# Fewer unread products ahead of one pair's scores, a third rectified tile, and scaling and reciprocal set apart, in a top-k attention kernel with a highway layer

## The chip, the cores and the metric

The kernel runs on one core of one Trainium2 chip. The metric is the device time of one execution in microseconds (us). Before the change it is 817.38 us, the median of three runs (813.4, 817.38 and 819.01). A core has five engines that work side by side, each through its own list of instructions: TensorE (PE in the profile; PEld is its weight load), VectorE (DVE), ScalarE (ACT), GpSimd (POOL) and SyncE (SP), which here only issues DMAs. They wait for one another through semaphores.

## The reference

There are 8 batches of 8 heads, 576 rows, head width 64. Each score row keeps its 32 largest entries, goes through a softmax, and is multiplied with the values. The heads of a row then form a vector of 512, which goes through a highway layer.

```python
scores = scale * np.matmul(q, k.transpose(0, 1, 3, 2))
kth = np.partition(scores, -top_k, axis=-1)[..., -top_k:-top_k + 1]
scores = np.where(scores >= kth, scores, -1000000000.0)
scores = scores - np.max(scores, axis=-1, keepdims=True)
attn = np.exp(scores)
attn = attn / (np.sum(attn, axis=-1, keepdims=True) + 1e-09)
x = np.matmul(attn, v)                    # then heads side by side: 4608 x 512
H = np.maximum(x @ w_h, 0.0)
T = 1.0 / (1.0 + np.exp(-(x @ w_t + b_t)))
out = T * H + (1.0 - T) * x
```

## The kernel before, in words

**Units, pairs and blocks.** The 576 rows of a batch are four full tiles of 128 rows and a last one of 64. A unit is one head of a full tile, or two heads of the last rows, stacked to 128 partitions. Two units make a pair, 18 pairs a batch: 16 of full tiles (numbers 0 to 15) and 2 of the last rows (16 and 17). There are 144 pairs in all. Four pairs make a full block, 128 rows of all eight heads; the two last-row pairs make one block of half the width.

**A step.** `step(i)` writes out, engine by engine, what is done in step i; each engine works through its instructions in the order in which they are written. Several pairs are in flight. In step i:

- PE adds the mask to the scores of pair i (`mask_add`, L409), multiplies the masked weights of pair i−3 with the values (`values`, L493), issues `spare(8)` (L277), and then the scores of pair i+2 (`scores`, L308 and L317 for full tiles, L325 and L334 for last rows). Behind these come part of a block's projections (`project`, L521, L523, L531) or transposes of the next batch's inputs (L249), and `spare(4)` or `spare(10)`.
- DVE takes the maxima of segments of pair i+1 (`segs`, L352), then the remaining maxima of pair i (`below`, L419, twice). Then it narrows the threshold down (`refine`, from L365 to L381), finds the 32nd value (L425, L438), and makes the masked weights of pair i−1 in `masked(0)` (L449) and `masked(1)` (L459, or L464 without help of POOL).
- ACT makes the comparison of one unit of the pair before (L442), may rectify or gate a projection (L606, L630) or copy transposes (L250), copies the accumulator out (`xs_copy`, L507), makes the exponentials (L415), copies scores (L347), and makes the masks (L396), which need the threshold of L381.
- POOL multiplies the hits (L435), makes biases (`biases`, L390) and one comparison (L453), and takes from a queue `pool_work` the scaling of a block (L562), two additions (L607, L608) and a product (L621). It issues DMAs: values for the next batch, casts of a block (L579), and `do_add` (L691), which adds the product tile to the sum of L607 by an accumulating DMA.
- SP issues the transposing DMAs of masked weights (L480) and of blocks (L584), loads and stores.

**Unread products.** `spare(n)` issues n products of constants into a part of the accumulator tile that nobody reads. The tile, `pso`, has one buffer: once four units' values are in it, `back_xs` has ACT copy it out and takes the tile anew, and the next products into it wait for that copy. `po["n"]` is the number of columns filled, 0 right after a copy.

**Scores.** Their PSUM tile has two buffers, so the scores of pair i+2 overwrite those of pair i, which DVE reads last in the second L419 of step i.

**The rectified tile.** `hh()` projects a block and writes the rectified result with ACT into the tile `h2` (named `h` in the profile). POOL uses it at L607 and L608, the product at L621 writes into it, and the accumulating DMA of L691 reads it. It comes from a pool of two buffers.

**Scaling and reciprocal.** When a block's heads are complete, `norm()` is put in the list `norms`, and `step` calls it at the end, behind `masked(1)` and the biases: DVE scales the sums (L556) and takes the reciprocal in place (L557). It also puts the block's scaling by L562 into `pool_work`. The biases of POOL are held behind `masked(1)` by an explicit dependence (`after`). A second path behind the main program, with exact maxima, runs only when a check at the end asks for it; it calls `norm()` too (L1099).

Of the kernel before, what the change touches and what calls it, by code (L numbers as in the profile page):

```python
# [11 lines left out]
FP32 = mybir.dt.float32  # L12
# [14 lines left out]
def kernel(  # L27
# [11 lines left out]
    P = nc.NUM_PARTITIONS  # L39
    B, H, S, D = q.shape  # L40
    dm = H * D
# [5 lines left out]
    nfull = S // P  # L47
# [11 lines left out]
    units = []  # L59
# [7 lines left out]
    pairs = [(u, u + 1) for u in range(0, NU, 2)]  # L67
    NG = len(pairs)
# [8 lines left out]
    etpool = ctx.enter_context(tc.tile_pool(name="et", bufs=6))  # L77
    xpool = ctx.enter_context(tc.tile_pool(name="x", bufs=3))
    fpool = ctx.enter_context(tc.tile_pool(name="f", bufs=2))
    xps = ctx.enter_context(tc.tile_pool(name="xps", bufs=2, space=bass.MemoryType.PSUM))  # L80
    ops = ctx.enter_context(tc.tile_pool(name="ops", bufs=1, space=bass.MemoryType.PSUM))
    fps = ctx.enter_context(tc.tile_pool(name="fps", bufs=1, space=bass.MemoryType.PSUM))
# [190 lines left out]
    def spare(n):  # L273
        if "t" not in po:
            po.update(t=pso_tile(), n=0)
        for _ in range(n):
            nc.tensor.matmul(  # L277
                po["t"][:, 4 * DE : BANK],
                ident_b[:],
                cst[:, 0 : BANK - 4 * DE],  # L280
                start=True,
                stop=True,
                skip_group_check=True,
            )
# [218 lines left out]
    def pso_tile():  # L503
        return ops.tile([P, BANK], FP32, tag="po", name="pso")
# [9 lines left out]
    def shape_of(qt):  # L514

        return (H, n_g, dm) if qt < nfull else (H // 2, n_g // 2, dm // 2)
# [31 lines left out]
    def ffn_pieces(b, qt, xs):  # L548
        nh, ng, w = shape_of(qt)
        st = dict(b=b, qt=qt, xs=xs)  # L550
        blocks.append(st)

        def norm():
            xs3 = xs[:, 0 : nh * DE].rearrange("p (h e) -> p h e", e=DE)
            rinv = cpool.tile([P, H], FP32, name="rinv")
            nc.vector.tensor_scalar(rinv[:, 0:nh], xs3[:, :, D], 1e-9, 2.0, ALU.add, ALU.mult)  # L556
            nc.vector.reciprocal(rinv[:, 0:nh], rinv[:, 0:nh])  # L557
            x = xpool.tile([P, dm], FP32, name="x")
            st["x"] = x

            def scaled(e):
                e.tensor_tensor(  # L562
                    x[:, 0:w].rearrange("p (h d) -> p h d", h=nh),
                    xs3[:, :, 0:D],
                    rinv[:, 0:nh].unsqueeze(2).to_broadcast([P, nh, D]),
                    ALU.mult,
                )
                if by_dma:
                    casts.append(cast)
                else:  # L570
                    ready.extend([xt, hh, tt])

            pool_work.append((scaled, w))

        by_dma = isinstance(b, int) and units[-1][0:2] > (b, qt + 2)

        def cast():
            xb = xpool.tile([P, dm], BF16, name="xb")
            nc.gpsimd.dma_start(xb[:, 0:w], st["x"][:, 0:w])  # L579
            return partial(turn, xb)  # L580

        def turn(xb):
            st["xT"] = fpool.tile([P, n_g, P], BF16, name="xT")
            nc.sync.dma_start_transpose(st["xT"][:, 0:ng, :], xb[:, 0:w])  # L584
            flying.append(b)
            ready.extend([hh, tt])

        def xt():
            ps = fps.tile([P, 512], FP32, tag="fp", name="fp")
            for g in range(ng):  # L590
                nc.tensor.transpose(ps[:, g * P : (g + 1) * P], st["x"][:, g * P : (g + 1) * P], ident_f[:])
            xT = fpool.tile([P, n_g, P], BF16, name="xT")
            st["xT"] = xT
            psv = ps[:].rearrange("p (g j) -> p g j", j=P)
            return lambda: nc.scalar.copy(xT[:, 0:ng, :], psv[:, 0:ng, :])

        def hh():
            ps = fps.tile([P, 512], FP32, tag="fp", name="fp")
            project(ps, qt, st["xT"], wh, False)
            h2 = fpool.tile([P, dm], FP32, name="h2")  # L600
            s1 = xpool.tile([P, dm], FP32, name="s1")
            st["h2"], st["s1"] = h2, s1
            x = st["x"]

            def evac():
                nc.scalar.activation(h2[:, 0:w], ps[:, 0:w], AF.Relu)  # L606
                pool_work.append((lambda e: e.tensor_add(s1[:, 0:w], h2[:, 0:w], x[:, 0:w]), w))  # L607
                pool_work.append((lambda e: e.tensor_sub(h2[:, 0:w], h2[:, 0:w], x[:, 0:w]), w))  # L608

            return evac  # L610

        def tt():
            ps = fps.tile([P, 512], FP32, tag="fp", name="fp")
            project(ps, qt, st["xT"], wt, True)
            if by_dma:
                flying.pop()
            t = fpool.tile([P, dm], FP32, name="tt")
            h2, s1 = st["h2"], st["s1"]

            def gated(e):  # L620
                ins = e.tensor_mul(h2[:, 0:w], h2[:, 0:w], t[:, 0:w])  # L621
                if e is nc.gpsimd:
                    adds.append((s1[:, 0:w], h2[:, 0:w], partial(store, b, qt, s1)))
                else:
                    e.tensor_add(s1[:, 0:w], s1[:, 0:w], h2[:, 0:w])
                    store(b, qt, s1)
                return ins

            def evac():
                nc.scalar.activation(t[:, 0:w], ps[:, 0:w], AF.Tanh)  # L630
                pool_work.append((gated, w))

            return evac

        return norm
# [21 lines left out]

    def blk_diff(k, ps):
        w = shape_of(k["qt"])[2]
        k["d"] = fpool.tile([P, dm], FP32, name="h2")  # L660
        nc.vector.scalar_tensor_tensor(
            out=k["d"][:, 0:w], in0=ps[:, 0:w], scalar=0.0, in1=k["x"][:, 0:w], op0=ALU.max, op1=ALU.subtract
        )
# [35 lines left out]
    norms = []  # L699
# [41 lines left out]
    po = {}  # L741
# [30 lines left out]
    def step(i):  # L772
# [31 lines left out]
        if back:  # L804
            back_pv(j)
            back_xs(j)
            st.pop(j)
        spare(8)
        ev = prep_filler() if to_prep and (i <= SPB or (len(to_prep) > 15 - k_in or len(layers) > 2) and i % 2) else None
        do_work(nc.gpsimd, 2 * dm if prev and ps_["r"][1] is None else dm)  # L810
        segs(i + 1, 2 * NSEG)
# [25 lines left out]
        def masked(s):  # L837
            if not prev:
                return None
            u = pu[s]  # L840
            if ps_["r"][s] is not None:
                ep, ins = (keep_min, keep_mul)[s](u, ps_["e"][s], ps_["r"][s])
            else:
                ep, ins = keep(u, ps_["sc"][s], ps_["e"][s])
            ps_["et"][s] = transposes(ep)
            return ins
# [20 lines left out]
        masked(0)  # L867
        for _ in ra:
            pass
        last = masked(1)  # L870
        if live:
            after(biases(i + 1), last)
        if norms:
            norms.pop(0)()
        if nxt:
            masks_of(i + 1)
        while turns and turns[0][0] <= i and len(flying) < 2:
# [166 lines left out]
    with tc.If(fine < 1):  # L1044
        with tc.For_i(0, B, 1) as bi:
# [26 lines left out]
            for pr in pairs[0 : NG // B]:  # L1072
                scs = copy_scores(scores(pr, prep)[2])
                ets = []
                for s, u in enumerate(pr):
                    b, qt, heads = units[u]
                    if heads[0] == 0:
                        xs = xpool.tile([P, H * DE], FP32, name="xs")
                    sc = scs[s]
                    w = cpool.tile([P, 32], FP32, name="gw")  # L1080
                    cur = sc
                    for r in range(TOP_K // 8):
                        nc.vector.max(w[:, r * 8 : r * 8 + 8], cur)
                        if r < TOP_K // 8 - 1:
                            nxt = gpool.tile([P, S], FP32, tag="gs", name="gs")
                            nc.vector.match_replace(nxt[:], w[:, r * 8 : r * 8 + 8], cur, -3.0e38)
                            cur = nxt[:]
                    nc.vector.tensor_copy(kth(u), w[:, TOP_K - 1 : TOP_K])
                    nc.vector.tensor_scalar_mul(tb(u), w[:, 0:1], -scale)
                    ep, _ = keep(u, sc, expo(u, sc))  # L1090
                    ets.append(transposes(ep))
                pso = pso_tile()
                n, r0 = values(pr, ets, vb, pso, 0), row_of(pr)
                if units[pr[0]][1] < nfull:
                    xs_copy(units[pr[0]][2][0], n, pso, xs)
                else:
                    xs_copy(0, n, pso, xs, r0, r0 + P2)
                if heads[-1] == H - 1:
                    ffn_pieces(bi, qt, xs)()  # L1099
                    do_work(nc.vector, NG * dm)  # L1100
                    while ready:
                        ready.pop(0)()()
                        do_work(nc.vector, NG * dm)
# [30 lines left out]
```

## Time and profile before

| | us |
|---|---|
| median of three runs | 817.38 |
| lowest and highest | 813.4 and 819.01 |
| the profiled execution, its own time | 818.4 |
| its span, first to last instruction | 816.7 |
| POOL busy | 559.3 |
| idle time of PE ahead of L277, for the copy of L507 | 40.0 in 70 waits |

The granted clock of TensorE was 0.993 of full speed over the span. A row of a timeline gives the start in us, the duration, engine and line, the tiles as out<-in, how many instructions are merged, and in brackets the idle time of the engine before the first and what ended it. A row of the chain gives the start, the duration and what ran; the chain is followed back from the last instruction to whatever released each one. A row of the waits reads "who <- whom: total us, times, longest".

### The profile page before, as it was taken

Reading aid. Unit: us, or ns where it says so; the run is one execution under the profiler, and the core shown is the slowest. Engines: PE = TensorE matmul, PEld = TensorE weight load, DVE = VectorE, ACT = ScalarE, POOL = GpSimd, SP = SyncE. Lnnn points to the kernel's source line nnn. Section 1 sums busy time; section 2 is a strip of 40 time slices with the busy share of each in tenths; the row PEclk is TensorE's granted clock in tenths of the full one; section 3 lists DMA queues with packets and bytes.
Section 4 is the critical chain, followed back from the end, with each engine's and each line's share of the span. In section 5 each row is a group of like instructions: output and inputs, shape, how many; then the busy total and the mean of one; then the engine's idle time right before and its main releaser. Section 6 shows DMA issues by size and latency. Waiting matters only on the chain.

```text
span 816.7 us, 20679 instructions
## 1 busy us (share of the span) xinstructions
PE 694.4 (85%) x6405; PEld 500.2 (61%) x6499; DVE 776.2 (95%) x4020; ACT 758.8 (93%) x1401; POOL 559.3 (68%) x712
## 2 busy tenths in 40 slices
PE   7889988888878888888888888888888888888884
PEld 5666766566655666566665666556656566565562
DVE  6999999999999999999999999999998999998995
ACT  5999999999999999999999998999999999998984
POOL 2666867777677766787667777677776776675750
PEclk9999999999999999999999999999999999999998
DMA  6799957985798657997679866697767975565553
GB/s 121 85 147 155 130 117 136 156 130 80 146 150 145 108 94 137 152 137 115 101 149 147 127 110 117 134 157 126 107 122 128 163 114 92 94 110 96 101 93 87
DMA packets 346359, 100.37 MB, mean 123 GB/s; under 512 B 330624, under 2 KB 338432, under 8 KB 346240
## 3 DMA queue, kind: packets, MB, share of 16 engines
q1 hardware_dynamic: 291024, 79.16, 53.0%
q0 software_dynamic: 53536, 19.34, 22.4%
q8 instruction: 53, 0.87, 0.4%
q10 hardware_dynamic: 1680, 0.46, 0.3%
q14 instruction: 66, 0.54, 0.2%
HBM read 31.72 MB, written 9.44 MB: 50 GB/s over the span
## 4 chain that ended last, share of the span: by engine, by line
ACT 37%; DVE 31%; PE 23%; DMA 4%; issue 3%; POOL 2%; SPq 0%; ACTq 0%; DVEq 0%; POOLq 0%
ACT m L396 14%; DVE wall L419 10%; DVE cand L352 9%; ACT e L415 7%; PE pso L277 6%; ACT sc L347 6%; ACT r L442 4%; PE xs L325 4%; DVE ep L449 3%; PE xs L308 3%; PE pso L493 2%; ACT xs L507 2%; DMA s<-h 2%; PE xs L409 2%; PE fp L521 2%
## 5 line engine op out<-in xcount | busy, mean ns | idle before, releaser
L352 DVE MAX8 cand<-xs 128x8 f32<-128x96 f32 x1728 | 297.1, 246 | 13.4 <-PE xs L334 7.4
L277 PE MATMUL pso<-cst,ident_b 128*128 128x252 bf16 x1881 | 253.1, 274 | 42.4 <-ACT xs L507 40.0
L453 POOL TENSOR_SCALAR ro<-sc,wall 128x576 bf16<-128x576 f32 x135 | 232.6, 1723 | 0.0
L277 PEld LDWEIGHTS <-ident_b 128*128 128x128 bf16 x1881 | 178.1, 98 | 82.1 <-issue 49.1
L415 ACT ACTIVATE e<-sc,be 128x576 bf16<-128x576 f32 x288 | 226.0, 785 | 0.1
L419 DVE MAX8 wall<-xs 128x8 f32<-128x576 f32 x288 | 204.0, 748 | 11.5 <-PE xs L409 5.0
L308 PE MATMUL xs<-kT,qT 64*128 64x256 f32 x1024 | 146.1, 402 | 31.9 <-DVE high L365 28.3
L347 ACT COPY sc<-xs 128x1152 f32<-128x1152 f32 x144 | 160.8, 1116 | 0.7 <-DVE cand L352 0.6
L308 PEld LDWEIGHTS xs<-kT,qT 64*128 64x128 f32 x1024 | 93.5, 187 | 62.9 <-issue 38.1
L435 POOL TENSOR_TENSOR hit<-hit,wall 128x18 f32<-128x18 f32 x143 | 32.4, 226 | 137.0 <-DVE hit L425 129.4
L396 ACT ACTIVATE m<-xs,wall 128x576 int8<-128x576 f32 x144 | 107.3, 745 | 20.0 <-DVE wall L381 17.8
L396 ACT ACTIVATE m<-sc,wall 128x576 int8<-128x576 f32 x144 | 111.3, 773 | 0.0
L409 PE MATMUL xs<-m,ident_b 128*128 128x64 bf16 (+1 forms) x507 | 92.0, 274 | 21.4 <-ACT m L396 19.4
L442 ACT ACTIVATE r<-sc,be 128x576 bf16<-128x576 f32 x143 | 109.8, 768 | 0.0
L409 PEld LDWEIGHTS <-ident_b 128*128 128x128 bf16 x576 | 51.7, 98 | 49.8 <-issue 29.3
L493 PEld LDWEIGHTS <-et 128*128 128x128 bf16 (+1 forms) x1600 | 68.9, 100 | 19.3 <-issue 3.8
L493 PE MATMUL pso<-vb,et 128*128 128x65 bf16 (+1 forms) x1600 | 74.6, 194 | 4.9 <-DMA et<-ep 0.3
L390 POOL TENSOR_TENSOR be<-wall,fac 128x4 f32<-128x4 f32 x144 | 29.1, 202 | 71.3 <-DVE ep L459 42.4
L449 DVE TENSOR_TENSOR ep<-e,r 128x576 bf16<-128x576 bf16 x143 | 64.5, 451 | 0.2 <-ACT r L442 0.2
L317 PEld LDWEIGHTS xs<-kd,qT 128*128 128x128 f32 x256 | 38.1, 188 | 42.7 <-issue 42.2
L317 PE MATMUL xs<-kd,qT 128*128 128x128 f32 x256 | 62.5, 326 | 0.0
L459 DVE TENSOR_TENSOR ep<-e,ro 128x576 bf16<-128x576 bf16 x135 | 60.5, 448 | 0.0
(127 smaller groups left out, 1024.1 us busy)
## 6 DMA issues: line engine op xcount, KB each, us to landing
kin<-in_k_dram SPq DMA_DIRECT2D x64, 128.0 KB, 3.0
qin<-in_q_dram SPq DMA_DIRECT2D x62, 128.0 KB, 3.2
out_dram<-s SPq DMA_DIRECT2D x30, 256.0 KB, 2.8
s<-h POOLq DMA_DIRECT2D x29, 256.0 KB, 4.1
et<-ep SPq DMA_TRANSPOSE x286, 3.4
xb<-x POOLq DMA_DIRECT2D x30, 128.0 KB, 3.1
vb<-in_v_dram POOLq DMA_DIRECT2D x28, 128.0 KB, 4.7
vb<-in_v_dram POOLq DMA_DIRECT2D x24, 64.0 KB, 3.2
```

What stands on the lines that cost most here:

```text
L277: nc.tensor.matmul(po["t"][:, 4 * DE : BANK], ident_b[:], cst[:, 0 : BANK - 4 * DE], start=True, stop=True, skip_group_check=True,)
L308: nc.tensor.matmul(ps[:, mo + n0 : mo + n0 + 256], qT[r : r + D, hp, qs : qs + P], kT[r : r + D, hp, n0 : n0 + 256], start=(n0 == 0), stop ...
L317: nc.tensor.matmul(ends, qT[:, hp, qs : qs + P], kd[:, hp, :], start=True, stop=True)
L347: nc.scalar.copy(sc[:], both)
L352: nc.vector.max(cand[:, s, :], sc[:, s * SEG : (s + 1) * SEG])
L396: nc.scalar.activation(m1[:].bitcast(I8)[:, 1 : 2 * S : 2], ps, AF.Sign, bias=wall[:, u, THR : THR + 1], scale=ABOVE, accum_out=csum[:, u ...
L409: nc.tensor.matmul(ps[:, s0:s1], ident_b[:], m1[:, s0:s1], start=False, stop=True, skip_group_check=True)
L415: nc.scalar.activation(e[:], sc, AF.Exp, bias=tb(u), scale=scale)
L419: nc.vector.max(wall[:, u, THR + 1 : KTH], ps)
L442: nc.scalar.activation(r[:], sc, AF.Relu, bias=eb(u), scale=BIGK)
L453: nc.gpsimd.tensor_scalar(r[:], sc, kth(u), None, ALU.is_ge)
L493: nc.tensor.matmul(pso[r0 : r0 + ql, col : col + DE], ets[s][:, c, gi * P2 : gi * P2 + ql], vb[:, h, vc, :], start=(c == 0), stop=(c == nc ...
```

## The change

Three edits go together. The rectified tile gets a pool of its own with three buffers; the last blocks' difference tile (`blk_diff`) uses the same pool. In step i, three unread products are issued in place of eight when pair i+2 is a last-row pair and the accumulator has just been copied out (`po["n"]` is 0); everywhere else there are eight as before. And `norm()` becomes a generator with two stops: `step` runs it up to the scaling (L556) behind `refine` and ahead of `masked(1)`, and goes on with the reciprocal (L557) and the entry in `pool_work` behind the biases, where the whole stood before. The second path runs the generator to its end.

```diff
+    hpool = ctx.enter_context(tc.tile_pool(name="h", bufs=3))
...
             nc.vector.tensor_scalar(rinv[:, 0:nh], xs3[:, :, D], 1e-9, 2.0, ALU.add, ALU.mult)
+            yield
             nc.vector.reciprocal(rinv[:, 0:nh], rinv[:, 0:nh])
...
             pool_work.append((scaled, w))
+            yield
...
-            h2 = fpool.tile([P, dm], FP32, name="h2")
+            h2 = hpool.tile([P, dm], FP32, name="h2")
...
-        k["d"] = fpool.tile([P, dm], FP32, name="h2")
+        k["d"] = hpool.tile([P, dm], FP32, name="h2")
...
-        spare(8)
+        spare(8 if i + 2 >= NG or units[pairs[i + 2][0]][1] < nfull or po["n"] else 3)
...
+        scaling = norms.pop(0)() if norms else iter(())
+        next(scaling, None)
         last = masked(1)
         if live:
             after(biases(i + 1), last)
-        if norms:
-            norms.pop(0)()
+        next(scaling, None)
...
-                    ffn_pieces(bi, qt, xs)()
+                    for _ in ffn_pieces(bi, qt, xs)():
+                        pass
```

## The prediction

> **What bounds the kernel now.** I read the page first (busy times, chain), then the waits, then the timelines of VectorE (DVE), ScalarE (ACT) and TensorE (PE) at the places that the change touches.
>
> ```profile
> span 816.7 us, 20679 instructions
> PE 694.4 (85%) x6405; PEld 500.2 (61%) x6499; DVE 776.2 (95%) x4020; ACT 758.8 (93%) x1401; POOL 559.3 (68%) x712
> ACT 37%; DVE 31%; PE 23%; DMA 4%; issue 3%; POOL 2%; SPq 0%; ACTq 0%; DVEq 0%; POOLq 0%
> ```
>
> Two engines are nearly full, and the chain runs through three. So work that is cut, or a wait that is lifted, counts only where the chain passes at that moment; elsewhere the other full engine gives the gain back. The waits say where there is something to win:
>
> ```profile
> ACT m L396 <- DVE wall L381: 17.8, 41, 1.8
> ...
> DVE cand L352 <- PE xs L334: 7.4, 15, 0.6
> PE fp L521 <- DMA xT<-xb: 6.9, 9, 2.3
> ...
> ACT h L606 <- DMA s<-h: 6.7, 4, 1.9
> ...
> DVE wall L419 <- remote: 4.4, 4, 1.3
> ```
>
> (Columns: total us, times, longest.) In 41 of some 144 steps ACT waits for DVE before its masks; in the others it is ACT, or PE behind it, that sets the pace. Row two is DVE waiting for the scores of the last-row pairs, row three PE waiting for a block's transposed tile; rows four and five are ACT held by the buffer of the rectified tile, and DVE held behind ACT in the same four steps.
>
> **Part 1: the third rectified tile.** With two buffers, the rectification at L606 must wait until the accumulating DMA that reads the tile of two blocks before has landed. That binds four times, once in each of batches 4 to 7. The second of them: the chain, the accumulating DMA before that one, ACT, DVE:
>
> ```profile
> 505.65 4.68 DMA s<-h
> ...
> 510.41 0.60 ACT h L606
> ...
> 513.36 1.48 ACT m L396 x4
> ```
>
> ```profile
> 483.28 0.92 POOL L691 DMA_DIRECT2D s<-h  x1 [0.26 <-POOL hit L435]
> ```
>
> ```profile
> 510.41 0.60 ACT L606 ACTIVATE h<-fp 128x512 f32<-128x512 f32 x1 [1.89 <-DMA s<-h]
> ```
>
> ```profile
> 511.65 0.20 DVE L381 TENSOR_REDUCE wall<-cand 128x4 f32<-128x32 f32 x1
> ...
> 515.39 1.43 DVE L419 MAX8 wall<-xs 128x8 f32<-128x576 f32 x2 [1.19 <-remote]
> ```
>
> ACT stood 1.89 us before 510.41. With a third buffer the wait is on a tile one block older, whose DMA was issued at 483.28, 22 us earlier; landing took 4.68 us in the chain's row, so nothing is left of it. What is late next: the mask at 513.36 also needs L381, done 0.20 us after 511.65, so the masks can move up at most 1.5 us, less than the 1.89. DVE then no longer waits the 1.19 us at 515.39, because the mask path moves further than that. So each of the four places is worth DVE's own wait, not ACT's: together the 4.4 us of the last row above, not the 6.7 of ACT's. The ends: nothing, if another wait takes over in all four, and 6.7. I take 4.4, since both engines' rows stand there. POOL's additions and the DMA keep their place; the change gives POOL nothing, and nothing queued behind them gets later.
>
> At the third of the four places there is more. PE sat idle while ACT waited, and its clock then fell (the stretches with the first rival):
>
> ```profile
> 614.35 1.84 PE L277 MATMUL pso<-cst,ident_b 128*128 128x252 bf16 x8 [0.47 <-ACT xs L507]
> ```
>
> ```profile
> 618.48 0.76 DVE L352 MAX8 cand<-xs 128x8 f32<-128x96 f32 x4 [1.35 <-PE xs L317]
> ```
>
> Eight products that take 1.02 us elsewhere (below) took 1.84, and DVE waited 1.35 us for the scores behind them. Without the wait PE isn't idle there: 1.35 us more in this execution. Part 1: 5.75 us.
>
> **Part 2: three products, not eight.** The condition holds once in a batch, eight times in all: pair 14 of 18, where the accumulator was just copied out and the scores that follow are those of a last-row pair. The second of the eight: the chain, PE, DVE:
>
> ```profile
> 188.83 1.02 PE pso L277 x8
> ```
>
> ```profile
> 189.78 1.08 PE L325 MATMUL xs<-kT,qT 64*64 64x256 f32 x8
> ```
>
> ```profile
> 189.34 0.18 DVE L365 TENSOR_TENSOR high<-cand 128x48 f32<-128x48 f32 x1
> ...
> 192.00 1.74 DVE L352 MAX8 cand<-xs 128x8 f32<-128x96 f32 x10 [0.44 <-PE xs L334]
> ```
>
> Eight cost 1.02 us, so five are 0.64. But the scores can't follow at once: they overwrite the PSUM tile that the second L419 reads, and L365 is the next instruction of DVE behind it. Where nothing stands before the scores, they begin 0.23 us behind L365; that is the case in the next step, with the other last-row pair:
>
> ```profile
> 97.59 0.18 DVE L365 TENSOR_TENSOR high<-cand 128x48 f32<-128x48 f32 x1
> ```
>
> ```profile
> 97.82 0.43 PE L325 MATMUL xs<-kT,qT 64*64 64x256 f32 x2
> ```
>
> Above they begin at 189.78, 0.44 behind, so 0.21 us can be won, not 0.64. The first and the last of the eight:
>
> ```profile
> 91.40 0.18 DVE L365 TENSOR_TENSOR high<-cand 128x48 f32<-128x48 f32 x1
> ```
>
> ```profile
> 92.04 0.65 PE L325 MATMUL xs<-kT,qT 64*64 64x256 f32 x4
> ```
>
> ```profile
> 780.84 0.18 DVE L365 TENSOR_TENSOR high<-cand 128x48 f32<-128x48 f32 x1
> ```
>
> ```profile
> 781.04 0.65 PE L325 MATMUL xs<-kT,qT 64*64 64x256 f32 x4
> ```
>
> Read in the same way, the eight starts lie 0.64, 0.44, 0.51, 0.45, 0.44, 0.44, 0.43 and 0.20 us behind their L365: gains of 0.41, 0.21, 0.28, 0.22, 0.21, 0.21, 0.20 and 0, together 1.7 us. The ends: 0 and 5.1 us (eight times 0.64); I take 1.7, by rows of the same places. All eight groups of products lie on the chain, so it counts in full. What hides the remaining idle time of DVE there is nothing: 0.2 us stay at each place, as PE needs over 2 us for these scores.
>
> **Part 3: scaling and reciprocal apart.** L556 moves ahead of the masked product of the second unit, L557 stays behind it. There are 38 blocks.
>
> ```profile
> 116.13 0.17 DVE L556 TENSOR_SCALAR rinv<-xs 128x8 f32<-128x8 f32 x1
> 116.33 0.20 DVE L557 RECIPROCAL rinv<-rinv 128x8 f32<-128x8 f32 x1
> 116.45 0.38 DVE L352 MAX8 cand<-xs 128x8 f32<-128x96 f32 x2
> ```
>
> From L556 to L557, which needs its result, are 0.20 us, more than its 0.17. An instruction of this size that the next doesn't wait for costs less from start to start: in the rows of L365 and L367 at 510.32 and 510.43, 0.11 us, though the first lasts 0.19.
>
> ```profile
> 510.32 0.19 DVE L365 TENSOR_TENSOR high<-cand 128x48 f32<-128x48 f32 x1
> 510.43 0.20 DVE L367 TENSOR_TENSOR low<-cand 128x48 f32<-128x48 f32 x1
> ```
>
> So the split saves about 0.10 us each time. The ends are 0 and 38 times 0.20, 7.6 us (both whole instructions hidden is excluded, L557 keeps its 0.12). Of the 38, L557 lies on the chain at 7 (50, 116, 170, 214, 247, 268 and 762 us). The first and the last:
>
> ```profile
> 50.31 0.20 DVE rinv L557
> ```
>
> ```profile
> 761.68 0.20 DVE rinv L557
> ```
>
> At the four steps behind the lifted waits DVE becomes the bound, that makes 11: 1.1 us. At the rest ACT or PE sets the pace, and the gain is idle time. What is made later: the second masked product by the 0.09 to 0.12 us of L556, with it its transposing DMA on SP (its values are used three steps later) and the biases on POOL, behind which POOL's comparison and the queued additions start. The next transposed block on SP stands behind that DMA too; PE waited 9 times for such a block (the third row of the waits), so at most 9 times 0.1 us come back. I count nothing for it.
>
> The Trainium skill, "VectorE: DVE Perf Modes", section "The DRAIN you can't avoid", says that after each operation the next cannot issue until the pipe is empty, and that a semaphore between them costs nothing extra. By that rule part 3 would be worth 0, and the sum 1.1 us smaller. The trace disagrees for these small operations: 0.11 us between two that last 0.19.
>
> **Sum.** 5.75 + 1.7 + 1.1 = 8.55 us. The profiled execution took 818.4 us, 1.0 more than the median of the three runs: 818.4 − 8.55 = 809.85. Against the median it would be 808.8. I say 809.4, between the two, as the 1.35 us of the clock need not be in every run before.
>
> **Rivals.**
> *Slower: the unread products keep PE's clock up, and with fewer it falls.* Three stretches of 3.4 us, after the first of them the one that followed it, and last the stretch ahead of the second of the eight places (columns: us, busy time of PE, PEld, DVE, ACT, POOL, clock, DMA, GB/s):
>
> ```profile
> 610.90:614.30 3.40, 1.42 (x23) 1.10 (x24) 2.26 (x10) 3.28 (x9) 1.96 (x2) 1.00 0.58 115
> 614.30:618.30 4.00, 3.95 (x19) 2.52 (x19) 2.79 (x16) 4.00 (x8) 2.52 (x4) 0.57 0.44 76
> 737.20:740.60 3.40, 1.13 (x6) 0.70 (x8) 2.77 (x17) 2.46 (x6) 3.01 (x4) 1.00 0.75 100
> 511.90:515.30 3.40, 1.75 (x15) 1.23 (x16) 2.31 (x13) 3.40 (x7) 2.69 (x3) 1.00 0.65 136
> 187.40:190.80 3.40, 2.64 (x31) 1.90 (x33) 3.40 (x20) 3.40 (x6) 2.90 (x4) 1.00 0.91 75
> ```
>
> Behind 610.9 the clock was 0.57 of full speed (half of it for most of the 4 us), and behind 737.2 products of one shape took twice their time again; behind 511.9 they did not. So it falls somewhere between 1.42 and 1.75 us of work in 3.40. The last, less 0.64, is 2.0 and stays above. If it fell at all eight, each would cost 1.35 us (the row at 618.48) to 2.2 (these scores at half speed), say 1.8: 14.4 us, part 2 gone, 818.4 − 6.85 + 14.4 = 826. It decides from four places on. Chance 0.06. The Trainium skill, "TensorE: Matmul & The Clock Gate", section "HAM oscillation — how this bites in real kernels", names a gap of over 3.4 us without work as what lowers the clock; by that alone no drop would be here, and it would leave the sum as it is. The trace disagrees: 1.42 us of work in 3.40 was too little at 610.9.
>
> *The waits move on.* ACT comes earlier, but the gain is lost at the next block's transposed tile or at POOL, which is no faster: then 818.4 − 1.7 − 1.1 = 815.6. For it: POOL's late additions are what the DMA waited for. Against: after each of the four places the chain goes on through ACT and PE for over ten microseconds. Chance 0.21.
>
> *The split does nothing,* because L557 or L459 takes up the 0.10 us: 818.4 − 7.45 = 810.95. Against it are the rows of L365 and L367. Chance 0.10.
>
> *More goes than I count.* Behind the stretch of 737.2, too, DVE waited:
>
> ```profile
> 742.54 1.43 DVE L419 MAX8 wall<-xs 128x8 f32<-128x576 f32 x2 [2.53 <-PE xs L409]
> ```
>
> PE stood there waiting for a transposed tile. If the shifted timing spares that, up to 2.53 us more go: 807.3. Chance 0.15.
>
> **How the numbers follow.** My forecast has 0.48. Within 1% (about what a measurement of this kernel can tell from no change) means 809.2 to 825.6. Faster: the 0.15 and some six tenths of the forecast, as 809.4 lies on the border, 0.44; slower, the clock, 0.06; the rest 0.50. The runs before lie 5.6 us apart, so the range is the cases from 807.3 to 815.6, a little wider at the low end: 805 to 816.
>
> **What would show it.** Right: no row of ACT at L606 waiting for the DMA of s, the four waits of DVE at L419 named "remote" gone; L325 0.23 us behind L365 at all of the eight places, DVE's idle time before L352 there 0.2 us; L459 ahead of L557 with about 0.1 us from L556 to L459; no half-clock stretch near 614. Wrong: a row of the same length at L630 or L521, half-clock stretches at the eight places, or DVE's busy time and the span unmoved.

## The result, and the profile after

| | before | after |
|---|---|---|
| median, us | 815.94 (4 runs, 813.4 to 819.01) | 807.09 (4 runs, 806.17 to 807.69) |
| ratio, 95% interval | | 0.9895 [0.9865, 0.9925] |
| the profiled execution, own time / span | 818.4 / 816.7 | 806.17 / 804.5 |
| DVE busy | 776.2 | 772.8 |
| granted clock of TensorE | 0.993 | 0.996 |

The changed kernel is faster by 1.05%, with an interval of 0.75 to 1.35%, so it lies on the border of 1% that the prediction named, as the prediction's 809.4 did. Of all executions behind this document, two of the kernel before and one with the three products alone took 3.5 to 3.8 ms; no ratio rests on them, and their cause is not known. A second set of six runs, later, gave 807.17 us and 0.9889 [0.9864, 0.9914]. The profiled executions are 12.2 us apart, more than the medians (8.85), because the one of before is 2.5 us above its median and the changed one 0.9 below. Line numbers are one higher from 80 on, two or three higher from 558 on: L353 was L352, L366 L365, L420 L419, L460 L459, L559 L557, L609 L606. "The four places" below are those of the rectified tile, "the eight places" those of the three products.

The page of the changed kernel: its span, the busy times, and the chain.

```profile
span 804.5 us, 20583 instructions
...
PE 686.7 (85%) x6369; PEld 494.7 (61%) x6459; DVE 772.8 (96%) x4020; ACT 757.2 (94%) x1401; POOL 559.9 (70%) x712
...
ACT 37%; DVE 32%; PE 23%; DMA 4%; issue 3%; SPq 1%; another core or an unknown queue 0%; DVEq 0%; ACTq 0%
```

The chain has nearly the same shares as before; POOL's 2% is gone from it. PEld shows 40 weight loads fewer, five at each of eight places. DVE is 3.4 us less busy; the other 8.8 us of the span are idle time of DVE that is gone. Where, the waits of the changed kernel tell (who <- whom: total us, times, longest):

```profile
ACT m L397 <- DVE wall L382: 17.1, 47, 1.0
...
PE fp L522 <- DMA xT<-xb: 6.3, 8, 1.7
DVE cand L353 <- PE xs L335: 6.2, 15, 0.5
...
DVE wall L420 <- PE xs L410: 3.5, 8, 1.3
```

The two rows of the rectified tile, "ACT h <- DMA s<-h" and "DVE wall <- remote", aren't there any more. PE's wait for the transposed tile hardly changed (6.9 before), and eight waits of DVE for PE at L420 stand where five stood. ScalarE's timeline at the second of the four places shows the rectification without a wait; DVE's shows what is left at the first three of them (at the fourth nothing is left):

```profile
505.29 0.60 ACT L609 ACTIVATE h<-fp 128x512 f32<-128x512 f32 x1
```

```profile
408.22 1.43 DVE L420 MAX8 wall<-xs 128x8 f32<-128x576 f32 x2 [1.02 <-PE xs L410]
...
505.75 1.43 DVE L420 MAX8 wall<-xs 128x8 f32<-128x576 f32 x2 [0.16 <-PE xs L410]
...
602.31 1.43 DVE L420 MAX8 wall<-xs 128x8 f32<-128x576 f32 x2 [0.28 <-PE xs L410]
```

Before, these four waits were 0.81, 1.19, 1.14 and 1.25 us, 4.39 in all; 1.46 are left. The 1.02 at the first place has a new cause, which PE's timeline of the changed kernel names (the last row answers to the wait of 2.27 us before the 2.53 at 742.54):

```profile
406.39 0.81 PE L522 MATMUL fp<-wh,xT 128*128 128x512 bf16 x3 [1.31 <-DMA xT<-xb]
...
439.60 0.81 PE L522 MATMUL fp<-wh,xT 128*128 128x512 bf16 x3 [1.68 <-DMA xT<-xb]
...
728.82 0.81 PE L522 MATMUL fp<-wh,xT 128*128 128x512 bf16 x3 [0.62 <-DMA xT<-xb]
```

PE waits 1.31 us for a transposed tile; the masks of that step, and DVE behind them, wait with it. So at one of the four places the wait did move on, to a landing.

The scaling and the reciprocal, in DVE's timeline of the changed kernel:

```profile
404.51 0.20 DVE L382 TENSOR_REDUCE wall<-cand 128x4 f32<-128x32 f32 x1
404.63 0.16 DVE L557 TENSOR_SCALAR rinv<-xs 128x8 f32<-128x8 f32 x1
404.70 0.45 DVE L460 TENSOR_TENSOR ep<-e,ro 128x576 bf16<-128x576 bf16 x1
405.07 0.20 DVE L559 RECIPROCAL rinv<-rinv 128x8 f32<-128x8 f32 x1
405.18 2.02 DVE L353 MAX8 cand<-xs 128x8 f32<-128x96 f32 x12
```

From the scaling to the next instruction are 0.07 us, where they were 0.20 to the reciprocal. That is 0.13 us a block, 4.8 in 38 blocks. DVE's busy time shows 3.4 of it; the rest was idle time between the two instructions (0.03 us in the rows at 116.13 and 116.33 before).

Last, the second of the eight places, DVE and PE:

```profile
188.55 0.18 DVE L366 TENSOR_TENSOR high<-cand 128x48 f32<-128x48 f32 x1
...
190.90 1.25 DVE L353 MAX8 cand<-xs 128x8 f32<-128x96 f32 x7 [0.27 <-PE xs L335]
```

```profile
188.03 0.48 PE L278 MATMUL pso<-cst,ident_b 128*128 128x252 bf16 x3 [0.69 <-ACT xs L508]
188.68 1.08 PE L326 MATMUL xs<-kT,qT 64*64 64x256 f32 x8 [0.16 <-DVE wall L420]
```

The scores now begin 0.13 us behind L366 (0.44 before) and wait for DVE, not for the products. DVE's wait there went from 0.44 to 0.27. No stretch of half clock stands near 614 or 740, nor anywhere else ahead of the program's end.

### The profile page after: what moved, and what is told of

The parts are those of the page before. It is cut to its first block, busy times and chain, and to the rows that moved or that the text cites. A ratio compares the mean times of both kernels' runs of the same rounds, so it can differ in the third digit from the quotient of the medians.

```text
span 804.5 us, 20583 instructions
## 1 busy us (share of the span) xinstructions
PE 686.7 (85%) x6369; PEld 494.7 (61%) x6459; DVE 772.8 (96%) x4020; ACT 757.2 (94%) x1401; POOL 559.9 (70%) x712
## 4 chain that ended last, share of the span: by engine, by line
ACT 37%; DVE 32%; PE 23%; DMA 4%; issue 3%; SPq 1%; another core or an unknown queue 0%; DVEq 0%; ACTq 0%
ACT m L397 15%; DVE wall L420 12%; DVE cand L353 9%; ACT e L416 7%; ACT sc L348 6%; PE pso L278 5%; ACT r L443 4%; PE xs L309 4%; PE xs L326 3%; DVE ep L450 3%; DMA xT<-xb 3%; PE fp L522 3%; PE xs L410 3%; PE pso L494 2%; ACT xs L508 2%
## 5 line engine op out<-in xcount | busy, mean ns | idle before, releaser
L353 DVE MAX8 cand<-xs 128x8 f32<-128x96 f32 x1728 | 297.5, 248 | 11.4 <-PE xs L335 6.2
L278 PE MATMUL pso<-cst,ident_b 128*128 128x252 bf16 x1841 | 246.8, 272 | 42.8 <-ACT xs L508 40.4
L278 PEld LDWEIGHTS <-ident_b 128*128 128x128 bf16 x1841 | 173.4, 98 | 81.4 <-issue 49.5
L420 DVE MAX8 wall<-xs 128x8 f32<-128x576 f32 x288 | 204.3, 751 | 5.6 <-PE xs L410 3.5
L410 PE MATMUL xs<-m,ident_b 128*128 128x512 bf16 (+1 forms) x512 | 92.7, 274 | 17.3 <-ACT m L397 15.2
L410 PEld LDWEIGHTS <-ident_b 128*128 128x128 bf16 x576 | 51.7, 97 | 44.8 <-issue 24.1
L460 DVE TENSOR_TENSOR ep<-e,ro 128x576 bf16<-128x576 bf16 x135 | 60.7, 449 | 0.0
```

Source lines behind the costliest of these rows:

```text
L278: nc.tensor.matmul(po["t"][:, 4 * DE : BANK], ident_b[:], cst[:, 0 : BANK - 4 * DE], start=True, stop=True, skip_group_check=True,)
L353: nc.vector.max(cand[:, s, :], sc[:, s * SEG : (s + 1) * SEG])
L410: nc.tensor.matmul(ps[:, s0:s1], ident_b[:], m1[:, s0:s1], start=False, stop=True, skip_group_check=True)
L420: nc.vector.max(wall[:, u, THR + 1 : KTH], ps)
```

## The experiments

Two theories about the sum were open. By the first, the three edits take away different waits, and the prediction's terms (5.75, 1.7, 1.1) add up. By the second, tile and products take away the same waits or the same falls of the clock, so that each is worth more alone and less on top of the other. Each ratio is against the kernel before, run on the same chip in the same rounds; a gain in us is worked out from it with 817 us.

**One part alone: the third tile.**

```diff
+    hpool = ctx.enter_context(tc.tile_pool(name="h", bufs=3))
-            h2 = fpool.tile([P, dm], FP32, name="h2")
+            h2 = hpool.tile([P, dm], FP32, name="h2")
```

> The kernel before with the third rectified tile alone; eight products and the whole normalization stay. Theory A (the three gains add up, each in its own stretch): 5.75 us less than before, 4.4 where the clock did not fall in the run before; no wait of ACT at the rectification for the accumulating DMA, the four waits of DVE of about 0.8 to 1.25 us behind it gone. Theory B (the tile makes the whole gain and the other two edits are lost to the other engines): 8.9 us less, as with all three. Theory C (what the tile saves is the clock, not the wait): about 1.35 us less, with the waits of DVE replaced by others of the same length.

Measured: 811.53 us, 0.992 [0.9889, 0.9951], 6.5 us less than before (4.0 to 9.1 by the interval). DVE's waits in this kernel:

```profile
DVE cand L353 <- PE xs L335: 7.3, 15, 0.6
DVE wall L420 <- PE xs L410: 4.6, 2, 3.5
```

At the four places DVE doesn't wait at all: the 4.4 us are gone in full, and so is the half clock at 614. Two long waits are left at L420, both behind a late transposed tile: 1.07 us near 244, and 3.49 us near 737, where PE waits 2.67 us and the clock falls at 732.8. The second is the place of before's 2.53, a little worse. The interval reaches the 8.9 us of theory B; these waits, gone in the changed kernel or shorter there, speak against it.

**One part alone: three products.**

```diff
-        spare(8)
+        spare(8 if i + 2 >= NG or units[pairs[i + 2][0]][1] < nfull or po["n"] else 3)
```

> The kernel before with three unread products in place of eight at the eight places alone. Theory A: 1.7 us less than before; DVE's idle time ahead of the first segment maximum of the first last-row pair falls from 0.44 to about 0.23 us. Theory B: within 0.5 us of before, since ACT takes the 0.2 us back in the steps behind. Clock rival: half-clock stretches at these places and a time up to 6 us longer.

Measured: 812.44 us, 0.9936 [0.9915, 0.9956], 5.2 us less (3.6 to 6.9 by the interval), three times the 1.7 of the prediction. Its waits:

```profile
DVE wall L419 <- PE xs L409: 3.9, 6, 1.5
ACT h L606 <- DMA s<-h: 3.6, 3, 1.4
...
DVE wall L419 <- remote: 0.4, 1, 0.4
```

At the eight places DVE's waits went from 3.06 us in all to 0.95: 2.1, near the 1.7. The rest is elsewhere: no half clock near 614 or 740, the 2.53 us at 742 gone, and of the "remote" waits 0.4 left, though ACT still waits for the DMA. In their place DVE waits 1.46 us at 443.94 and 0.88 at 410.36 for PE, which waits for transposed tiles.

**One part alone: the split.**

```diff
+        scaling = norms.pop(0)() if norms else iter(())
+        next(scaling, None)
         last = masked(1)
...
-        if norms:
-            norms.pop(0)()
+        next(scaling, None)
```

> The kernel before with scaling and reciprocal apart alone; two rectified tiles, eight products. Theory A: 0.7 us less than before (seven blocks on the chain), from start to start of the scaling and the instruction behind it 0.1 us instead of 0.20. Theory B: within 0.5 us of before in time, though the 0.1 us is seen on DVE. If the split saves at all 38 blocks: 3.8 us less.

Measured: 816.39 us, 0.997 [0.9947, 0.9993], 2.4 us less (0.6 to 4.3, above theory B's 0.5, but not enough to part 0.7 from 3.8). The rectified tile has a pool of its own here, with two buffers as before. DVE's busy time is 773.6 us, 2.6 under before's. But the wait for the last-row scores grew:

```profile
DVE cand L353 <- PE xs L335: 8.4, 16, 0.8
```

It was 7.4. At the eight places DVE comes 0.13 us earlier and waits 0.13 us longer (0.57 for 0.44 at most of them), as the scores, not DVE, set the pace there. So about 1 us of the gain is given back.

**After, with eight products again** (`spare(8)` as before).

> The changed kernel with eight unread products again at the eight places (third tile and split stay). Alone, the three products had saved 5.2 us, where the sum counted 1.7. Theory A (the products are worth what DVE's idle time at the eight places shows, 1.7 to 2.1 us): about 2 us slower than the changed kernel, so 6.5 to 7 us less than before. Theory D (the shift that they make also moves the transposed block tiles off slow landings, above all the one near 735 us, for which PE waited 2.3 to 2.7 us with eight products and 0.6 with fewer, and spares the half-clock stretch behind it): 4 to 5 us slower than the changed kernel, so 4 to 5 us less than before, with the wait of over 2 us in that place again.

Measured: 808.73 us, 0.9908 [0.9878, 0.9938]: 1.1 us more than after's 0.9895 by the ratios, 1.6 by the medians, below the 4 to 5 that the second theory of the expectation wanted. The two intervals overlap, so that the difference isn't nothing is shown by the waits and not by the time. In DVE's timeline two things came back, the wait at the eight places (the second of them shown) and one near 730, but no half clock with them:

```profile
191.52 0.59 DVE L353 MAX8 cand<-xs 128x8 f32<-128x96 f32 x3 [0.57 <-PE xs L335]
...
731.74 1.43 DVE L420 MAX8 wall<-xs 128x8 f32<-128x576 f32 x2 [1.97 <-PE xs L410]
```

**After, with scaling and reciprocal together again** (the call of `norm()` where it stood).

> The changed kernel with scaling and reciprocal together again behind the biases. Alone, the split had saved 2.4 us, where the sum counted 0.7 and all 38 blocks would give 4.75. Theory A (only blocks on the chain count): about 1 us slower than the changed kernel. If DVE is the bound at half of the blocks and more: 2.4 us or more slower. The 0.2 us from scaling to reciprocal are back.

Measured: 808.45 us, 0.9909 [0.9877, 0.994], 1.1 us more than after by the ratios, again inside the intervals. DVE is busy 775.6 us, 2.8 more than after, and waits 0.14 us instead of 0.27 at the eight places: 1 of the 2.8 is cover for that wait.

**After, with two rectified tiles** (`bufs=2` in the tile's own pool).

> The changed kernel with two rectified tiles in place of three; three products at the eight places and the split stay. If the tile is worth what the prediction gave it (5.75 us), this kernel takes about 5.75 us more than the changed one: ratio to before about 0.9965. If the gains of tile and products overlap (alone they made 6.5 and 5.2 us, with the split 2.4, all three 8.6), the tile on top of the other two is worth 8.6 less 5.2 and 2.4, about 1 to 3 us: ratio 0.990 to 0.993, and VectorE's waits named remote make under 1 us in all.

Measured: 810.02 us, 0.9911 [0.9886, 0.9935]; after itself in the same rounds 807.17 and 0.9889. The third tile is worth 1.8 to 2.9 us on top of the other two, against 6.5 alone. So the gains overlap, as by the second theory. One detail of the expectation came out in name only: ACT's wait for the DMA is back, 4.9 of the 6.7 us, but none of DVE's waits is named "remote"; they are put down to PE, which stands behind ACT.

```profile
DVE wall L420 <- PE xs L410: 8.6, 13, 1.5
...
ACT h L609 <- DMA s<-h: 4.9, 4, 1.6
```

DVE's waits at L419/L420 of over 0.06 us, added up by place from the timelines, show the overlap:

| DVE waits, us | before | tile alone | products alone | split alone | after, eight | after, together | after, two tiles | after |
|---|---|---|---|---|---|---|---|---|
| four places of the rectified tile | 4.4 | 0 | 2.7 | 3.8 | 0.6 | 1.3 | 3.8 | 1.5 |
| behind a late tile near 242 or 317 | 1.4 | 1.1 | 1.1 | 1.7 | 0 | 0.3 | 1.3 | 0.5 |
| behind the tile near 440 | 0.9 | 0.2 | 1.5 | 0.6 | 0.4 | 1.2 | 1.5 | 1.3 |
| behind the tile near 735 | 2.5 | 3.5 | 0 | 3.4 | 2.0 | 0.1 | 0.2 | 0.2 |

With the tile alone the first row is empty and the last stays; with the products alone the last is empty and the third grows. Neither adds to the other in full. Besides, the half clock at 614 is lifted by either edit alone (with the split alone it stands at 416.7 instead).

The clock granted to each execution shows the same overlap. In 51 runs of the kernel before it lies between 0.986 and 0.997, and the time goes with it: 814.1 us (the median of six) at 0.996, 819.2 (of five) at 0.990. A straight line through the 51 gives 0.78 us for a thousandth, 1.6 us for one stretch of half clock of 3.4 us. An estimate from this line, with each run of a kernel set against before at the same granted clock: tile 4.1 to 4.5, products 2.5 to 2.9, split 1.2 to 1.6, together 7.8 to 9.0, and the changed kernel 6.9 to 8.3 (the ranges allow for the chips, which lie up to 0.7 us off the line). So where the clock is the same the three gains nearly add up, and much of the overlap would be falls of the clock, which the tile or the products lift alone too. No run tests this apart.

**No product at the eight places.**

```diff
-        spare(8 if i + 2 >= NG or units[pairs[i + 2][0]][1] < nfull or po["n"] else 3)
+        spare(8 if i + 2 >= NG or units[pairs[i + 2][0]][1] < nfull or po["n"] else 0)
```

> The changed kernel with no unread product, in place of three, at the eight places. Theory A (behind the cut DVE's last read of the scores' buffer sets their start): the same time as the changed kernel within 0.5 us, scores still about 0.23 us behind the first instruction of the narrowing. If the three products still stand in the way: 0.38 us less at each of eight places, 3 us. If PE's clock falls with so little work ahead of the scores (under some 1.6 us of 3.4): half-clock stretches there and 1.35 us or more at each place where it does.

Measured: 809.8 us, 0.990 [0.9866, 0.9935], with runs from 806.3 to 815.1: 806.3 to 808.9 at a granted clock of 0.996 or more, 810.7 to 815.1 at 0.990 or less. The profiled execution has a span of 812.3. In it the clock fell at four of the eight places. The fifth place in PE's timeline, DVE's wait behind it, and the 3.4 us ahead of the scores there and at the first place, where it didn't fall (columns as in the prediction):

```profile
480.37 1.68 PE L326 MATMUL xs<-kT,qT 64*64 64x256 f32 x8 [1.44 <-DVE high L366]
```

```profile
484.22 0.93 DVE L353 MAX8 cand<-xs 128x8 f32<-128x96 f32 x5 [1.99 <-PE xs L335]
```

```profile
87.81:91.21 3.40, 2.32 (x28) 1.71 (x25) 3.40 (x17) 3.26 (x8) 3.14 (x3) 1.00 1.30 151
476.97:480.37 3.40, 1.59 (x20) 1.16 (x20) 3.40 (x17) 3.40 (x9) 2.60 (x3) 1.00 0.91 134
```

The scores take 1.68 us for 1.08, and DVE waits 1.99 us (1.77 to 2.03 at the four), where it waits 0.34 at the places of full clock: the prediction's first rival, at a price of 1.4 to 1.7 us each, inside its 1.35 to 2.2. The three products, then, do hold the clock. In the changed kernel the like stretch at the second place has 2.04 us of work:

```profile
185.28:188.68 3.40, 2.04 (x22) 1.18 (x20) 3.40 (x17) 3.40 (x9) 3.14 (x3) 1.00 1.24 112
```

**No product in this place in any step** (`spare(0)`).

> The changed kernel with no unread product in this place in any step (those behind the scores stay). With none at the eight places alone PE's clock fell at four of them, 1.77 to 2.03 us of DVE's time each. If it is the share of work in a stretch of 3.4 us that counts: many half-clock stretches, tens of us slower than before. If the clock falls only at gaps of about 1.4 us ahead of last-row scores, as there: at most eight such stretches and about the time of the kernel with none at the eight places.

Measured: 816.39 us, 0.9999 [0.9971, 1.0028]: all the gain is lost. In the profiled execution the mean clock is 0.977 and there are seven stretches of half clock ahead of the end, the last of 10.2 us, and DVE waits for PE longer than in before at L420 and at the full tiles' segment maxima (5.0 and 3.6 us there):

```profile
DVE wall L420 <- PE xs L410: 10.0, 10, 3.5
DVE cand L353 <- PE xs L335: 6.8, 15, 0.5
DVE cand L353 <- PE xs L318: 6.2, 8, 1.8
```

**Three products after every copy, and five.** In the changed kernel most copies of the accumulator are still followed by eight.

```diff
-        spare(8 if i + 2 >= NG or units[pairs[i + 2][0]][1] < nfull or po["n"] else 3)
+        spare(8 if po.get("n", 1) else 3)
```

> The changed kernel with three unread products, in place of eight, after every copy of the accumulator (72 steps), not only ahead of the last-row pairs. Theory A (DVE's idle time ahead of the segment maxima in these steps, 0.12 to 0.25 us in some 20 of them, is what the products cost): 2 to 3 us less than the changed kernel. Clock rival (the work ahead of the scores then falls under some 1.6 us of 3.4): half-clock stretches at some of them, each 1.3 to 2 us, and a time above that of the changed kernel.

Measured: 804.72 us, 0.9854 [0.9823, 0.9885]. DVE's idle time ahead of the segment maxima of full tiles, past the first 20 us, fell from 4.0 to 0.8 us. The clock fell twice, at 24.6 and 120.1; the stretches ahead of both, and behind the second:

```profile
116.70:120.10 3.40, 1.35 (x10) 0.74 (x8) 3.29 (x21) 3.07 (x7) 2.99 (x4) 1.00 1.04 116
120.10:124.10 4.00, 4.00 (x34) 2.63 (x33) 1.46 (x4) 2.94 (x4) 0.84 (x1) 0.57 0.88 187
21.20:24.60 3.40, 1.74 (x14) 1.11 (x13) 3.03 (x15) 3.23 (x6) 2.04 (x5) 1.00 0.05 3
```

The same kernel a second time, and the changed kernel beside it:

> Three products after every copy, run a second time beside the changed kernel on the same chip. If its lead is real, it takes 0.985 of the time before and 2 to 4 us less than the changed kernel; if it came from the chip of that call, the two are within 1 us.

> The changed kernel itself, a second time, beside the three others: 0.9895 of the time before, between 0.9865 and 0.9925.

Measured: 806.06 us, 0.986 [0.9833, 0.9887], beside 807.17 and 0.9889 for the changed kernel. Both repeat their first ratio within 0.0006, and the clock fell twice again, at 24.8 and 789.4; the lead is 1.1 us by the medians and 2.4 by the ratios, below the expected 2 to 4 by the first. With five in place of three:

> Five products after every copy of the accumulator, in place of three after each (the earlier run took 0.9854 of the time before) or eight at most of them (the changed kernel, 0.9895). If the products only stand in the way of the scores, it lies between, about 0.987 to 0.988, with VectorE's idle time ahead of the segment maxima of full tiles between 0.8 and 4.0 us. If five are enough to hold the clock where three let it fall twice, it is at or under 0.9854, with no half-clock stretch.

Measured: 802.74 us, 0.9829 [0.9803, 0.9856], the fastest of all, 4.4 us under the changed kernel in the same rounds. No stretch of half clock ahead of the end, and idle time ahead of the full tiles' segment maxima of 0.5 us past the first 20 (1.1 of the 1.6 below lie in these 20): five are few enough for the scores and enough for the clock. The page and DVE's waits:

```profile
span 800.9 us, 20321 instructions
```

```profile
DVE wall L420 <- PE xs L410: 2.8, 8, 0.7
DVE cand L353 <- PE xs L318: 1.6, 3, 0.6
```

Part of its lead may be where the code is fetched, which the last section shows; these runs don't take the two apart.

## Why the prediction came out, and where it was wrong

The time lies in the range, 2.3 us under the forecast. By the profiled executions the sum was 8.55 us and 12.2 went; by the medians 8.85 went. The terms came out unequally, and that the sum is so near is in part luck: alone, each edit gave more than its term, 14.1 us in all, and the overlap, which the sum doesn't have, took some 5 back.

*Part 1, the tile, 5.75.* The mechanism is shown: with the tile alone the four waits of DVE, 4.4, are gone, not ACT's 6.7, and the half clock near 614 is gone too (6.5 us in all). The step that failed is that the term was added to the others. On top of products and split the tile is worth 1.8 to 2.9 us, and in the changed kernel 2.9 of the 4.4 went, because at the first place a late transposed tile binds instead. That is the rival "the waits move on" at one place in four.

*Part 2, the products, 1.7.* At the places themselves: 2.1 without the split (0.44 to 0.14 at most of them) and 2.3 with it (0.57 to 0.27; the row of DVE for L335 has 8.5 us with eight products and 6.2 after). The mis-sized step is the 0.23 us that was left behind L365; it is 0.13. At the third of the eight the forecast counted 0.28 where DVE had no wait that it could lose. What was not seen at all is that fewer products change the time by 5.2 us when they come alone, through clock and landings elsewhere; at the same granted clock the estimate above leaves 2.5 to 2.9.

*Part 3, the split, 1.1.* The sign holds alone, 2.4 us with 0.6 to 4.3 by the interval; the 1.1 by the ratios in company lies inside them. The working was off twice. The gain is 0.13 us a block, not 0.10. And at the eight last-row places it comes back as a wait for the scores, 1 us in all, which the prediction didn't name: with eight products or with three, the split wins nothing there. DVE's busy time falls by 2.6 to 3.4 us, in all 38 blocks whichever engine sets the pace; that 11 of them count is neither shown nor excluded. The rule of the Trainium skill's "VectorE: DVE Perf Modes", section "The DRAIN you can't avoid", by which the part would be worth nothing, doesn't hold for this pair: 0.07 us pass from the start of the scaling to the next instruction's start, while the scaling lasts 0.16. The section itself excepts a next operation "that is not held", which the prediction left out.

*The rivals.* The clock did not fall at three products; it does at none, at the price worked out. The 2.53 us at 742.54 went, as in the case "more goes": 2.35 of the profiled difference of 12.2. Whether every run of before has that wait is open; the four kernels of before's eight products that were profiled all have it.

*The signs.* All that were named as right are there but two: 0.13 in place of 0.23 behind L366, and DVE's idle time of 0.27 in place of 0.2. One of the signs of a wrong forecast is half there, the longer waits at L522 near 407 and 440.

## What to carry to other kernels

Two edits that lift waits of the same few microseconds are not added: each is measured with and without the other, since here 6.5, 5.2 and 2.4 us alone made 8.6 together. Filler work that holds a clock has a best amount, and it differs from both "as much as fits" and "none": here, with the tile and the split, eight in every step gave 808.7 us, five after each copy 802.7, three after each copy 804.7 to 806.1, and none in any step 816.4. A shorter instruction list also moves the moments at which code is fetched, and with them which transfers are late; before a wait for a landing is explained by the kernel, it is worth looking whether a fetch of code stands beside it.

## What the runs showed of the hardware

**A fetch of code delays a transposing DMA.** The queue rows in a stretch of some 4.3 us from the issue of one transposed tile to the end of PE's wait for it; "q8 instruction" and "q14 instruction" are fetches of code (packets, MB, share), and the last row has the median us from issue to landing. Before, and the changed kernel at the same tile:

```profile
q8 instruction: 1, 0.02, 1.4%
...
xT<-xb SPq DMA_TRANSPOSE x1, 4.1
```

```profile
q14 instruction: 1, 0.01, 0.6%
...
xT<-xb SPq DMA_TRANSPOSE x1, 2.5
```

The changed kernel at the tile issued at 402.18, for which PE waits at 406.39, and the changed kernel with eight products at the tile of the first two fences:

```profile
q8 instruction: 1, 0.02, 1.4%
q14 instruction: 1, 0.01, 0.7%
...
xT<-xb SPq DMA_TRANSPOSE x1, 3.9
```

```profile
q8 instruction: 1, 0.02, 1.5%
...
xT<-xb SPq DMA_TRANSPOSE x1, 4.2
```

With a fetch on q8 the tile lands in about 4 us, without one in 2.5. Over the traces of all 14 profiled executions, 518 such transfers: in 53 a packet of q8 starts within 2.1 us after the issue, and all 53 land after 3.3 us (median 4.1); of the other 465, 33 do (median 2.5), nine of them with a fetch that began up to 0.6 us ahead of the issue. The border is sharp: of 18 with a fetch 2.1 to 2.4 us behind the issue, two land so late. Fetches on q14 matter less: with one of these alone in the same 2.1 us, 10 of 63 land so late (median 2.85). At the tile near 735 the fetch starts 2.0 to 2.1 us after the issue in before, tile alone, split alone, eight products and no product in any step, and these five wait 2.3 to 2.7 us for it; in the nine others it starts 7 us behind or 3 ahead, and they wait at most 1 us.

This goes with the last row of the table above, and with the changed kernel's waits near 408 and 440, whose tiles have such a fetch 1.9 and 1.4 us behind their issue. The products move the fetch: in the changed kernel q8 fetches 53 times in 804.5 us, once in 15.2, and PE has 6459 weight loads with a product to each, 12,918 instructions, 244 to a fetch. Seven of the eight places lie ahead of 735; they drop 70 of these, 0.29 of a fetch, so as an estimate from these rows 4.4 us, and 5.1 was measured (7.1 behind the issue, against 2.0 with eight). That q8 serves PE is seen where the number of products changes: 51 fetches for 12,566 such instructions with five after every copy, 44 for 10,710 with none in any step, 243 to 246 to a fetch, while the counts of DVE, ACT and POOL stay the same. No run moved the fetch alone. The Trainium skill, "Runtime: NRT & Kernel Launch", section "Instruction fetch mechanics", says that code comes in blocks of 16 KiB and that crossing to the next is mostly hidden. The packets of q8 are of that size. No run here shows an engine waiting for its code; what the fetch costs here is another transfer's time, for which PE waited over 2 us.

**The clock falls without a long idle stretch.** With no products at the eight places it fell after PE had stood 1.44 us, with 1.59 us of work in 3.40. Together with the prediction's rows and those of the run with three products after every copy, it falls behind 1.13, 1.35, 1.42, 1.59 and once 1.74 us, and not behind 1.75, 2.04, 2.32 and 2.64: a share of work near one half. But one number taken just ahead of the scores doesn't decide: with no products at the eight places, 1.46 us of work lie in the 3.40 ahead of the scores of the second place (184.62 to 188.02), and the clock stayed.

What decides is shown by the moments of the changes. In the granted clock of all 14 profiled executions, each change lies a whole number of steps of 3.413 us behind the first one, to 1 ns. With PE's work added up step by step, all 34 falls, 14 of them at the programs' ends, stand behind a step with at most 1.76 us of work; of the 3211 other steps at full clock, five have 1.69 to 1.76 and the rest more. So the same stretch of little work is safe or not by where the steps cut it. The Trainium skill, "TensorE: Matmul & The Clock Gate", section "HAM oscillation — how this bites in real kernels", sees the risk in idle stretches of over 3.4 us; in the profiled executions with no product at the eight places, and with none in any step, PE was never idle for as long as 2.5 us, and the clock fell four and seven times ahead of the end.

**A dependent pair of small DVE instructions costs its wait.** 0.20 us from scaling to reciprocal, 0.07 from scaling to an instruction that doesn't need it.
